# A windowed attention feeding a SoLU layer: two more tiles computed as a pair, their first sums on another engine, constants in one load, the last product in two halves

## The chip, the cores and the metric

The kernel runs on one core of one Trainium2 chip. The metric is the device time of one execution in microseconds (us). A core has TensorE (PE, with its weight loads shown apart as PEld), VectorE (DVE), ScalarE (ACT), GpSimd (POOL) and SyncE (SP, which here only issues transfers). Each takes its instructions in the order in which they were written, and waits at semaphores for the others.

## The reference

Attention in windows over 8 batches x 8 heads x 576 positions of 64 numbers, then a two-layer net with softmax-gated units over the 4608 rows that come out of it.

```python
scores = scale * q @ k.T                       # per batch and head
mask_plain = (rel >= 0) & (rel < 32)           # first 4 heads
mask_dil = (rel >= 0) & (rel < 128) & (rel % 4 == 0)   # last 4 heads
attn = softmax(where(mask, scores, -1e9))
x = (attn @ v) as rows of 512                  # 4608 x 512
h = x @ w_in                                   # 512 -> 1024
solu = h * softmax(h)
ln = (solu - mean) / sqrt(var + 1e-6) * g_ln
out = ln @ w_out                               # 1024 -> 512
```

## The kernel before

**Units and tiles.** The attention is cut into 32 units (two heads of one batch each), the net into 36 tiles of 128 rows. `scores` (L247 for the mask on TensorE, L255 for q with k), the softmax and `attend` (L333) make a unit; its x goes, transposed and split into a high and a low part, to a ring `x_hi`, `x_lo`. Products are made of three matmuls (high x high, high x low, low x high) in fp32r.

**Tiles.** Tiles 0 to 15 are computed singly: `moe_h` (L401) takes 24 matmuls of 512 columns for h, then maximum, exponential, gate, centring, variance. The result goes to DRAM and comes back so that it can be turned (L508 on VectorE), split (L516 on ScalarE, L522 on GpSimd) and multiplied with w_out (`moe_o`, L531, 24 matmuls of 512 columns per tile). Tiles 16 to 35 go in pairs: seven products P1 to P7 (`product`, L733, six matmuls each) replace the eight blocks of two tiles' h. They need sums of blocks of w_in (made once, words `fa` to `fh`, split by `Th`, `Tl`) and four sums S1 to S4 of blocks of x for each pair (`sums`, words z1 to z4; split by `hS12`, `hS34`, `lS12`, `lS34`). While the pair's rows are still in the ring (`in_ring`, tiles up to 17), x has a high and a low part, and S1 to S4 take 4, 2, 3 and 2 instructions; later one each where no batch boundary lies in the tile.

**Order.** No scheduler: the order on every engine is written out as words. `OPENING` covers the conversion of the weights, the first 12 units and tiles 0 to 5. Then `STEP` runs for each single tile i from 6 on (a step is h of tile i, scores of unit i+4, attend of unit i+3, w_out for tile i-2), with the words of `AMID` put behind its three parts in some steps. `PAIRED` is the first tile that is paired; from there `PAIR`, `PAIR_ALONE` and `LAST_PAIR` give the words for each pair, which also hold two units' attention and w_out of the two tiles before. `engine` gives z1 to z4, lS12 and lS34 to GpSimd.

**Loads.** All loads are issued by SP, in the order of the words. Each transfer takes the next of eight semaphores, and waits until the transfer eight places ahead of it, which had the same one, has landed.

**The end.** `LAST_PAIR` ends with the product of tile 35 with w_out, its eviction with the scale `rstd` in two halves (L548 on ScalarE, L551 on VectorE) and two stores.

Of the kernel before, what the change touches and what calls it, by code (L numbers as in the profile page):

```python
# [130 lines left out]
def windowed_attention_then_solu_kernel(  # L131
# [7 lines left out]
    g_ln: bass.AP,  # L139
    mask: bass.AP,  # L140
    ident: bass.AP,
    ident_bf: bass.AP,
# [20 lines left out]
    id_sb = const.tile([P, P], F32, name="id_sb")  # L163
    mask_sb = const.tile([P, 2, NS * WQ], BF16, name="mask_sb")
    g_sb = const.tile([P, FT], F32, name="g_sb")
    id_bf = const.tile([P, P], BF16, name="id_bf")
# [373 lines left out]
    def moe_out(i):  # L540
        ob = moe.tile([P, DO], F32, name="ob", bufs=1)
        rows, rstd = out[i * P : i * P + P, :], ms[i]["rstd"]
        if i < NTILE - 1:
            nc.scalar.activation(out=ob, in_=ps_o(i), func=AF.Copy, scale=rstd)  # L544
            nc.sync.dma_start(out=rows, in_=ob)
        else:
            left, right = slice(0, DO // 2), slice(DO // 2, DO)
# [3 lines left out]
            nc.vector.tensor_scalar(  # L551
                out=ob[:, right], in0=ps_o(i)[:, right], scalar1=rstd, scalar2=None, op0=ALU.mult
            )
            nc.scalar.dma_start(out=rows[:, left], in_=ob[:, left])
            nc.sync.dma_start(out=rows[:, right], in_=ob[:, right])
# [414 lines left out]
```

## Time and profile before

| | us |
|---|---|
| median of 3 runs (501.88, 503.55, 503.7) | 503.55 |
| the profiled execution | 504.69 |
| its span, first to last instruction | 502.8 |
| PE busy | 469.9 |
| DVE busy | 351.4 |
| POOL busy | 298.7 |
| ACT busy | 291.3 |

The profile is of one execution, slower by 1.14 than the median, and its span is 1.89 shorter than its own time. Busy time is how long an engine had an instruction in work; PE's ends are modelled. The slices of the page show when: PE starts slowly (1, 4, 5, 7 tenths in the first four of 40 slices), and from the seventh slice on is at 9 tenths until the last, which has 6. The transfer engines have 7 to 9 tenths in the first four slices.

### The profile page before, as it was taken

What the parts mean: (1) busy time and instruction counts of PE and PEld (TensorE: products, weight loads), DVE (VectorE), ACT (ScalarE), POOL (GpSimd) and SP (SyncE); (2) the same over time, 40 slices, a digit from 0 to 9 for tenths busy, and PEclk for the clock granted to TensorE, in tenths of its full rate; (3) what the DMA queues carried; (4) which work ended last, traced back from release to release, by engine and by line L of the source; (5) the groups of instructions that cost most, each with busy time, mean ns of one, the idle gap of its engine ahead of it and who ended that gap; (6) DMA issues with size and microseconds to landing.
All of it is one profiled execution on the core that took longest, in us unless ns stands there. A gap on an engine that the chain in (4) does not pass through costs nothing.

```text
span 502.8 us, 16542 instructions
## 1 busy us (share of the span) xinstructions
PE 469.9 (93%) x7064; PEld 376.0 (75%) x7064; DVE 351.4 (70%) x619; ACT 291.3 (58%) x483; POOL 298.7 (59%) x367
## 2 busy tenths in 40 slices
PE   1457998999999999999999999999999999999996
PEld 1336776788878888788878787878787888888875
DVE  3996989867627788777868686868676865445562
ACT  3766897744424444534457575757575767666551
POOL 1652776556533765778976666665756555766440
PEclk9999999999999999999999999999999999999999
DMA  7979175664465655666667677676765545354461
GB/s 280 402 254 359 37 261 163 230 190 133 137 193 156 194 164 169 186 175 178 201 175 216 206 211 211 210 211 211 212 210 164 160 129 146 104 168 124 113 188 63
DMA packets 51337, 94.14 MB, mean 187 GB/s; under 512 B 5952, under 2 KB 26048, under 8 KB 51264
## 3 DMA queue, kind: packets, MB, share of 16 engines
q1 hardware_dynamic: 50544, 92.43, 59.6%
q8 instruction: 55, 0.90, 0.8%
q10 hardware_dynamic: 720, 0.66, 0.4%
q14 instruction: 18, 0.15, 0.1%
HBM read 60.04 MB, written 28.31 MB: 176 GB/s over the span
## 4 chain that ended last, share of the span: by engine, by line
PE 91%; DMA 5%; issue 2%; DVE 1%; ACT 0%; SPq 0%; DVEq 0%; ACTq 0%
PE banks L531 40%; PE banks L733 20%; PE banks L401 18%; PE banks L333 7%; PE banks L255 6%; DMA qt<-qT 2%; DMA raw<-w_in 2%; DMA kt<-kT 1%; DVE pt L317 0%; PE banks L247 0%; DVE x_lo L388 0%; DVE nmax L412 0%; SPq L232 0%; DVE rs L302 0%; ACT sm L285 0%
## 5 line engine op out<-in xcount | busy, mean ns | idle before, releaser
L531 PE MATMUL banks<-w_o,th 128*128 128x512 f32 x576 | 179.9, 393 | 0.0
L522 POOL TENSOR_TENSOR tl<-t,th 128x512 fp32r<-128x512 f32 x68 | 87.9, 1305 | 59.9 <-ACT th L516 59.8
L531 PEld LDWEIGHTS banks<-w_o,th 128*128 128x128 f32 x576 | 106.6, 188 | 22.6 <-ACT th L516 0.6
L531 PE MATMUL banks<-w_o,tl 128*128 128x512 f32 x288 | 112.5, 391 | 0.0
L401 PE MATMUL banks<-w_i,x_hi 128*128 128x512 f32 x256 | 82.8, 405 | 0.2 <-DVE mu L436 0.2
L531 PEld LDWEIGHTS banks<-w_o,tl 128*128 128x128 f32 x288 | 54.0, 188 | 12.3 <-DVE tl L522 0.9
L516 ACT CAST th<-t 128x512 fp32r<-128x512 f32 x72 | 43.4, 621 | 23.5 <-DVE t L508 16.1
L401 PEld LDWEIGHTS banks<-w_i,x_hi 128*128 128x128 f32 x256 | 47.2, 191 | 11.1 <-DVE mu L436 0.8
L508 DVE STREAM_TRANSPOSE t<-raw 128x512 f32<-128x512 f32 x72 | 46.9, 684 | 6.1 <-DMA out<-ob 3.0
L401 PE MATMUL banks<-w_i,x_lo 128*128 128x512 f32 x128 | 50.7, 396 | 0.0
L333 PEld LDWEIGHTS banks<-pt,vt 32*64 32x64 f32 x2816 | 35.3, 138 | 20.0 <-issue 12.8
L452 ACT ACTIVATE e<-t 128x1024 f32<-128x1024 f32 x35 | 37.0, 1058 | 17.6 <-DVE t L448 17.3
L294 POOL TENSOR_TENSOR sm<-sm,mx 128x640 f32<-128x640 f32 x27 | 34.5, 1276 | 21.4 <-DVE mx L281 18.8
L333 PE MATMUL banks<-pt,vt 32*64 32x64 f32 (+3 forms) x2816 | 38.8, 234 | 8.6 <-issue 5.4
L298 ACT ACTIVATE sm<-sm 128x640 f32<-128x640 f32 x32 | 23.6, 739 | 35.8 <-POOL sm L294 35.1
L255 PEld LDWEIGHTS banks<-kt,qt 64*32 64x32 f32 x2560 | 29.8, 112 | 17.7 <-issue 10.7
L269 DVE TENSOR_TENSOR sm<-banks,mask_sb 128x640 f32<-128x640 f32 x22 | 18.1, 824 | 35.1 <-PE banks L255 35.0
L255 PE MATMUL banks<-kt,qt 64*32 64x64 f32 x2560 | 35.7, 238 | 5.6 <-issue 4.1
L544 ACT ACTIVATE ob<-banks,rstd 128x512 f32<-128x512 f32 x35 | 24.0, 686 | 24.8 <-issue 16.6
L757 DVE CUSTOM_DVE_ANT_0 t<-banks,t 128x512 f32<-128x512 f32 x30 | 20.7, 690 | 22.3 <-PE banks L733 16.9
L751 ACT COPY t<-banks 128x512 f32<-128x512 f32 x30 | 17.6, 588 | 30.3 <-PE banks L733 30.3
L427 ACT ACTIVATE e<-t,nmax 128x1024 f32<-128x1024 f32 x19 | 21.9, 1153 | 18.8 <-DVE nmax L764 18.2
(151 smaller groups left out, 868.5 us busy)
## 6 DMA issues: line engine op xcount, KB each, us to landing
mid<-t SPq DMA_DIRECT2D x140, 128.0 KB, 2.4
raw<-mid SPq DMA_DIRECT2D x34, 512.0 KB, 3.9
vt<-vw SPq DMA_DIRECT2D x32, 384.0 KB, 3.9
kt<-kT SPq DMA_DIRECT2D x32, 312.0 KB, 4.4
qt<-qT SPq DMA_DIRECT2D x32, 296.0 KB, 4.7
out<-ob SPq DMA_DIRECT2D x35, 256.0 KB, 2.7
x_hi<-x SPq DMA_DIRECT2D x12, 288.0 KB, 3.5
t<-w_in SPq DMA_DIRECT2D x5, 512.0 KB, 7.8
```

What stands on the lines that cost most here:

```text
L255: nc.tensor.matmul(out=ps[WIN * c : WIN * c + WIN, h, WQ * i : WQ * i + WQ], lhsT=qt[D * h : D * h + D, q0 : q0 + WIN], rhs=kt[D * h : D * ...
L294: eng.tensor_tensor(out=st[n]["sm"], in0=st[n]["sm"], in1=wide(mx), op=ALU.subtract)
L298: nc.scalar.activation(out=sm, in_=sm, func=AF.Exp, scale=0.125)
L333: nc.tensor.matmul(out=ps_x[D * h : D * h + D, c, c0 : c0 + k1 - k0], lhsT=vt[WIN * c : WIN * c + WIN, i, D * h : D * h + D], rhs=pt[WIN * ...
L401: nc.tensor.matmul(out=ps_h(i)[:, half], lhsT=a[:, kt, xs], rhs=w_i[:, kt, half, part, :], start=(kt == 0 and k == 0), stop=(kt == KT - 1 ...
L452: nc.scalar.activation(out=e, in_=t, func=AF.Square, accum_out=per_tile(i, "sq"))
L508: nc.vector.transpose(out=turned(i)[:, cut(c)].rearrange("p k (a r) -> p k a r", r=WIN), in_=ms[i]["mv"].rearrange("p (a k s) -> p k a s", ...
L516: nc.scalar.copy(out=ms[i]["th"][:, cut(c)], in_=turned(i)[:, cut(c)])
L522: eng.tensor_tensor(out=ms[i]["tl"][:, cut(c)], in0=turned(i)[:, cut(c)], in1=ms[i]["th"][:, cut(c)].bitcast(F32), op=ALU.subtract,)
L531: nc.tensor.matmul(out=ps_o(i), lhsT=a[:, f, :], rhs=w_o[:, f, part, :], start=(f == 0 and k == 0), stop=(f == FT - 1 and k == 2), skip_gr ...
L544: nc.scalar.activation(out=ob, in_=ps_o(i), func=AF.Copy, scale=rstd)
L733: nc.tensor.matmul(out=banks[:, bank], lhsT=left(pa, kt), rhs=right(pb, kt), start=j in (1, 2, 5) and kt == 0 and k == 0, stop=kt == 1 and ...
```

## The change

Five things, in the numbers and words that set the order, and in two functions.

1. `PAIRED` goes from 16 to 14: steps 14 and 15 fall away, tiles 14 and 15 become a pair in front of the other pairs. Their rows are in the ring.
2. The words of `AMID` start in step 8 instead of 9 and end in step 13 instead of 15.
3. In `sums`, S1 and S2 of the first pair go to VectorE; those of all others stay on GpSimd.
4. Four constants (bf16 identity, two masks, gains) lie in one array `pack` and are loaded by one transfer instead of four; the fp32 identity, which nothing read, is gone.
5. The product of tile 35 with w_out is made in two halves of 256 columns (`moe_o_half`), into two banks; the left half is evicted and stored while the right one is computed, and the right half is evicted in two quarters.

```diff
-PAIRED = 16
+PAIRED = 14
...
 AMID = {
-    9: ("fa0 fb0 fc0", "Th0", ""),
-    10: ("fd0 fe0 ff0", "Th4 Tl4 Tl0", ""),
-    11: ("fg0 fh0", "Th2 Tl2 Th6 Tl6", ""),
-    12: ("fa1 fb1 fc1", "Th1", ""),
-    13: ("fd1 fe1 ff1", "Th5 Tl5 Tl1", ""),
-    14: ("fg1 fh1 z1.s z2.s", "Th3 Tl3 Th7 Tl7", ""),
-    15: ("z3.s z4.s", "hS12.s lS12.s", "hS34.s lS34.s back.i"),
+    8: ("fa0 fb0 fc0", "Th0", "fd0"),
+    9: ("fe0 ff0", "Th4 Tl4 Tl0", "fg0 fh0"),
+    10: ("", "Th2 Tl2 Th6 Tl6", "fa1 fb1 fc1"),
+    11: ("fd1 fe1 ff1", "Th1 Th5 Tl5 Tl1", ""),
+    12: ("fg1 fh1", "Th3 Tl3 Th7 Tl7", "z1.s z2.s"),
+    13: ("z3.s z4.s", "hS12.s lS12.s", "hS34.s lS34.s back.i"),
 }
...
-    "w1 ib abs1 w3 m0 low1 q0 clamp1 w0 sign1 w2 abs3 q1 low3 q2 join1 hi1 S0 sign3 clamp3 "
+    "w1 pack abs1 w3 low1 q0 clamp1 w0 sign1 w2 abs3 q1 low3 q2 join1 hi1 S0 sign3 clamp3 join3 "
...
-    "oA.b oB.b out.b "
+    "oL.b outL.b oR.b outR.b "
...
-        a, b, eng = 2 * r, 2 * r + 1, engine(f"z{j}")
+        a, b = 2 * r, 2 * r + 1
+        eng = nc.vector if a == PAIRED and j <= 2 else engine(f"z{j}")
...
+    packed = const.tile([P, P // 2 + NS * WQ + FT], F32, name="packed")
+    id_bf = packed[:, 0 : P // 2].bitcast(BF16)
...
+    def moe_o_half(i, half):
+        th, tl = ms[i]["th"], ms[i]["tl"]
+        cols = slice(DO // 2 * half, DO // 2 * half + DO // 2)
+        for f in range(FT):
+            for k, (a, part) in enumerate(((th, 0), (th, 1), (tl, 0))):
+                nc.tensor.matmul(
+                    out=banks[:, half, cols],
+                    lhsT=a[:, f, :],
+                    rhs=w_o[:, f, part, cols],
...
+    def out_left(i):
+        moe_out_part(i, 0, slice(0, DO // 2), True)
+
+    def out_right(i):
+        moe_out_part(i, 1, slice(DO // 2, DO * 3 // 4), True)
+        moe_out_part(i, 1, slice(DO * 3 // 4, DO), False)
```

`moe_out_part(i, half, cols, on_act)` evicts the columns with the scale and stores them: on ScalarE with ScalarE's own queue, or on VectorE with SP's.

The order at three places follows. A name's number is its buffer, or a running count behind it; in square brackets stand the semaphores that an instruction waits for. Those named DMAHW0 to DMAHW7 are the eight that the transfers take in turn.

SP in the opening, before. Ahead of these rows stand t1 (the first block of w_in), the bf16 identity and t3 (the second block), with DMAHW0 to DMAHW2; t0, t2, raw4 and raw5 are further blocks of w_in, kt and qt the keys and queries of a unit:

```order
L835 DMA mask_sb_81<-mask 128x320
L209 DMA kt0_109<-kT 128x624
L210 DMA qt0_108<-qT 128x592
L232 DMA t0_113<-w_in 128x1024
L232 DMA t2_116<-w_in 128x1024
L209 DMA kt1_121<-kT 128x624 [waits DMAHW0_49]
L210 DMA qt1_120<-qT 128x592 [waits DMAHW1_49]
L209 DMA kt2_127<-kT 128x624 [waits DMAHW2_49]
L210 DMA qt2_126<-qT 128x592 [waits DMAHW3_49]
L232 DMA raw4_178<-w_in 128x1024 [waits DMAHW4_49]
L835 DMA mask_sb_81<-mask 128x320 [waits DMAHW5_49]
L232 DMA raw5_190<-w_in 128x1024 [waits DMAHW6_49]
```

And in the changed kernel, behind t1 with DMAHW0:

```order
L857 DMA packed_80<-pack 128x392
L228 DMA t3_100<-w_in 128x1024
L205 DMA kt0_105<-kT 128x624
L206 DMA qt0_104<-qT 128x592
L228 DMA t0_109<-w_in 128x1024
L228 DMA t2_112<-w_in 128x1024
L205 DMA kt1_117<-kT 128x624
L206 DMA qt1_116<-qT 128x592 [waits DMAHW0_49]
L205 DMA kt2_123<-kT 128x624 [waits DMAHW1_49]
L206 DMA qt2_122<-qT 128x592 [waits DMAHW2_49]
L228 DMA raw4_174<-w_in 128x1024 [waits DMAHW3_49]
L228 DMA raw5_185<-w_in 128x1024 [waits DMAHW4_49]
```

`packed` stands second and the two mask loads are gone. kt1 waits for nothing now, kt2 for `packed` instead of t3, raw4 for kt0 as before, raw5 for qt0 instead of t0.

VectorE at the end of step 12, before: x of unit 15, the end of unit 16's softmax, then the turns of tile 11 (`raw5` to `t3`) and the mask of unit 17:

```order
L388 TENSOR_TENSOR x_lo_89<-banks_90,x_hi_88 128x576
L312 TENSOR_TENSOR sm0_3009<-sm0_3009,rs_3074 128x640
L317 STREAM_TRANSPOSE pt0_3104<-sm0_3009 128x640
L508 STREAM_TRANSPOSE t3_2883<-raw5_2943 128x512 x2
L269 TENSOR_TENSOR sm1_3200<-banks_90,mask_sb_81 128x640
L281 TENSOR_REDUCE mx_3202<-sm1_3200 128x10
```

And in the changed kernel, where `mag3` and `low3` are the low parts of two sums of w_in and `qt3` holds S1 and S2:

```order
L384 TENSOR_TENSOR x_lo_86<-banks_87,x_hi_85 128x576
L308 TENSOR_TENSOR sm0_3015<-sm0_3015,rs_3079 128x640
L313 STREAM_TRANSPOSE pt0_3109<-sm0_3015 128x640
L588 TENSOR_TENSOR mag3_3112<-vt3_2339,more_2714 128x512
L588 TENSOR_TENSOR low3_3116<-kt3_2218,last_3114 128x512
L591 TENSOR_TENSOR qt3_2220<-x_hi_85 128x256
L591 TENSOR_TENSOR qt3_2220<-qt3_2220,x_lo_86 128x256 x2
L588 TENSOR_TENSOR qt3_2220<-qt3_2220,x_hi_85 128x256
L588 TENSOR_TENSOR qt3_2220<-qt3_2220,x_lo_86 128x256
L504 STREAM_TRANSPOSE t3_2890<-raw5_2949 128x512 x2
L265 TENSOR_TENSOR sm1_3216<-banks_87,packed_80 128x640
```

Two low parts and six instructions for S1 and S2 have come between the softmax of unit 16 and the turns of tile 11.

ScalarE behind the last split, and VectorE's last instruction, before: `ob` is what is stored, PE, Activation, DVE and Pool are the engines' semaphores:

```order
L516 CAST th1_6856<-t3_6696 128x512 [waits DVE_49]
L544 ACTIVATE ob_6887<-banks_90,rstd_6813 128x512 [waits PE_49,DMAHW0_49,Activation_49,Pool_49]
L548 ACTIVATE ob_6914<-banks_90,rstd_6813 128x256 [waits DMAHW1_49,PE_49,Activation_49]
L554 DMA out<-ob_6914 128x256 [waits DMAHW2_49,Activation_49]
L551 TENSOR_SCALAR ob_6914<-banks_90,rstd_6813 128x256 [waits DMAHW0_49,DMAHW1_49,Activation_49,Pool_49]
```

And in the changed kernel:

```order
L539 ACTIVATE ob_6889<-banks_87,rstd_6815 128x512 [waits PE_49,DMAHW4_49,Activation_49,Pool_49]
L566 ACTIVATE ob_6916<-banks_87,rstd_6815 128x256 [waits DMAHW5_49,PE_49,Activation_49]
L567 DMA out<-ob_6916 128x256 [waits DMAHW6_49,Activation_49]
L566 ACTIVATE sm1_6943<-banks_87,rstd_6815 128x128 [waits PE_49]
L567 DMA out<-sm1_6943 128x128 [waits DMAHW7_49,Activation_49]
L569 TENSOR_SCALAR sm0_6946<-banks_87,rstd_6815 128x128 [waits Activation_49,Pool_49]
```

ScalarE has a left half and a quarter to evict, and VectorE's quarter waits for ScalarE's semaphore as its half did.

## Rows read from the trace of the kernel before

**Rows 1.** The page: the span, the busy time of each engine with its share and count of instructions (section 1), and the chain that ended last by engine (section 4).

```profile
span 502.8 us, 16542 instructions
...
PE 469.9 (93%) x7064; PEld 376.0 (75%) x7064; DVE 351.4 (70%) x619; ACT 291.3 (58%) x483; POOL 298.7 (59%) x367
...
PE 91%; DMA 5%; issue 2%; DVE 1%; ACT 0%; SPq 0%; DVEq 0%; ACTq 0%
```

**Rows 2.** The table of stages: from and to, length, then busy us and count of PE, PEld, DVE, ACT and POOL, granted clock, share of the transfer engines, GB/s.

```profile
12.00:26.40 14.40, 6.75 (x262) 4.51 (x261) 14.00 (x25) 10.80 (x18) 8.14 (x6) 1.00 1.03 402
26.40:42.90 16.50, 7.69 (x339) 6.17 (x339) 14.17 (x23) 8.97 (x15) 9.65 (x7) 1.00 0.84 286
...
62.00:82.00 20.00, 17.56 (x446) 13.58 (x448) 17.02 (x32) 17.15 (x30) 14.55 (x25) 1.00 0.69 216
...
140.00:254.00 114.00, 113.93 (x1833) 91.45 (x1831) 84.81 (x127) 51.64 (x87) 78.28 (x103) 1.00 0.61 181
254.00:404.00 150.00, 150.00 (x2547) 120.39 (x2545) 111.59 (x215) 95.09 (x159) 96.76 (x109) 1.00 0.66 197
```

**Rows 3.** The chain of work that ended last, in order of time, in the opening: start us, us, what.

```profile
17.39 9.02 DMA qt<-qT
...
26.97 2.98 issue
...
32.47 2.56 issue
...
38.61 2.83 issue
...
42.91 4.48 PE banks L401 x12
```

**Rows 4.** The timeline of the opening: start us, us, engine, line, instruction, and in brackets the idle time before it with what ended it.

```profile
1.17 0.42 SPq L833 DMA_DIRECT2D id_bf<-ident_bf  x1
...
8.58 0.33 SPq L209 DMA_DIRECT2D kt<-kT  x1
8.58 0.66 ACT L780 ACTIVATE mag<-t 128x512 f32<-128x512 f32 x1 [2.75 <-DMA t<-w_in]
...
11.65 0.33 SPq L232 DMA_DIRECT2D raw<-w_in  x1
...
14.00 0.69 PE L247 MATMUL banks<-mask_sb,id_bf 128*128 128x320 bf16 x2 [2.12 <-DVE sm L291]
```

**Rows 5.** The page, section 3: a DMA queue, its packets, MB and share of 16 engines. This is the queue that brings instructions.

```profile
q8 instruction: 55, 0.90, 0.8%
```

**Rows 6.** The chain again: two products of 320 columns, six products of a pair, and the 24 of one tile with w_out.

```profile
51.35 0.29 PE banks L247 x2
...
268.83 1.36 PE banks L733 x6
270.19 5.44 PE banks L531 x24
```

**Rows 7.** The table of stages, columns as in rows 2: step 12, step 15 and the first pair (tiles 16 and 17).

```profile
197.77:211.10 13.33, 13.33 (x210) 10.71 (x209) 11.16 (x18) 6.38 (x12) 9.59 (x12) 1.00 0.59 174
...
238.23:251.56 13.33, 13.33 (x210) 10.71 (x209) 11.29 (x18) 6.67 (x13) 12.05 (x19) 1.00 0.67 201
251.56:276.76 25.20, 25.20 (x428) 20.22 (x426) 18.51 (x37) 16.04 (x27) 17.46 (x20) 1.00 0.66 196
```

**Rows 8.** The timelines of single engines: VectorE and GpSimd in step 13, TensorE in step 13, then GpSimd and TensorE in the first pair.

```profile
211.76 1.26 DVE L508 STREAM_TRANSPOSE t<-raw 128x512 f32<-128x512 f32 x2
...
213.16 2.53 POOL L522 TENSOR_TENSOR tl<-t,th 128x512 fp32r<-128x512 f32 x2 [1.14 <-ACT th L516]
...
219.60 0.39 PE L531 MATMUL banks<-w_o,tl 128*128 128x512 f32 x1
...
264.42 2.56 POOL L522 TENSOR_TENSOR tl<-t,th 128x512 fp32r<-128x512 f32 x2 [1.49 <-ACT th L516]
...
270.48 0.39 PE L531 MATMUL banks<-w_o,tl 128*128 128x512 f32 x1
```

**Rows 9.** Groups of instructions by line and shape: count, then busy us and mean ns of one, then idle us before them.

```profile
L531 PEld LDWEIGHTS banks<-w_o,tl 128*128 128x128 f32 x288 | 54.0, 188 | 12.3 <-DVE tl L522 0.9
...
L544 ACT ACTIVATE ob<-banks,rstd 128x512 f32<-128x512 f32 x35 | 24.0, 686 | 24.8 <-issue 16.6 <-DMA out<-ob 4.2 <-PE banks L531 3.9
...
L564 DVE TENSOR_TENSOR vt<-x_hi,vt 128x256 fp32r<-128x256 f32 x6 | 4.4, 726 | 0.0
...
L567 POOL TENSOR_TENSOR kt<-kt,x_lo 128x256 f32<-128x256 f32 x2 | 1.5, 742 | 0.2
...
L564 DVE TENSOR_TENSOR mag<-vt,more 128x512 fp32r<-128x512 f32 x2 | 1.3, 652 | 0.0
...
L564 DVE TENSOR_TENSOR x_lo<-x_hi,x_lo 128x256 fp32r<-128x256 f32 x1 | 0.4, 383 | 0.0
```

**Rows 10.** The timeline of the end: two weight loads at the start of the last product, and the two evictions behind it.

```profile
492.77 0.30 PEld L531 LDWEIGHTS banks<-w_o,th 128*128 128x128 f32 x2 [0.17 <-ACT th L516]
...
498.90 0.47 ACT L548 ACTIVATE ob<-banks,rstd 128x256 f32<-128x256 f32 x1 [5.02 <-PE banks L531]
...
499.47 0.48 DVE L551 TENSOR_SCALAR ob<-banks,rstd 128x256 f32<-128x256 f32 x1 [5.43 <-ACT ob L548]
```

**Rows 11.** DMA issues of the whole run: KB each and median us from issue to landing.

```profile
out<-ob ACTq DMA_DIRECT2D x1, 128.0 KB, 1.8
```

More of the change, by code (lines that the diff above doesn't have):

```diff
@@ L138, in windowed_attention_then_solu_kernel @@
     w_out: bass.AP,
[L139 to L142, printed above, removed]
+    pack: bass.AP,
     out: bass.AP,
@@ L161, in windowed_attention_then_solu_kernel @@
     )
[L163 to L166, printed above, removed]
+    packed = const.tile([P, P // 2 + NS * WQ + FT], F32, name="packed")
+    id_bf = packed[:, 0 : P // 2].bitcast(BF16)
+    mask_sb = packed[:, P // 2 : P // 2 + NS * WQ].bitcast(BF16).rearrange("p (d c) -> p d c", d=2)
+    g_sb = packed[:, P // 2 + NS * WQ :]
     mhalf = const.tile([P, 1], F32, name="mhalf")
@@ L542, in moe_out @@
         rows, rstd = out[i * P : i * P + P, :], ms[i]["rstd"]
-        if i < NTILE - 1:
-            nc.scalar.activation(out=ob, in_=ps_o(i), func=AF.Copy, scale=rstd)
-            nc.sync.dma_start(out=rows, in_=ob)
-        else:
-            left, right = slice(0, DO // 2), slice(DO // 2, DO)
-            nc.scalar.activation(
-                out=ob[:, left], in_=ps_o(i)[:, left], func=AF.Copy, scale=rstd
-            )
[L551 to L555, printed above, removed]
+        nc.scalar.activation(out=ob, in_=ps_o(i), func=AF.Copy, scale=rstd)
@@ new lines, in moe_out @@
+        nc.sync.dma_start(out=rows, in_=ob)
+        del ms[i]
+    def moe_o_half(i, half):
[7 more added lines that the diff above has]
+                    rhs=w_o[:, f, part, cols],
+                    start=(f == 0 and k == 0),
+                    stop=(f == FT - 1 and k == 2),
+                    skip_group_check=True,
+                )
@@ new lines, in moe_out_part @@
+    def moe_out_part(i, half, cols, on_act):
+        if half == 0:
+            ob = moe.tile([P, DO], F32, name="ob", bufs=1)
+        else:
+            ob = att.tile([P, 2, NS, WQ], F32, name=f"sm{int(on_act)}")
+            ob = ob.rearrange("p h s w -> p (h s w)")
+        rows, rstd = out[i * P : i * P + P, :], ms[i]["rstd"]
+        ps = banks[:, half]
+        if on_act:
+            nc.scalar.activation(out=ob[:, cols], in_=ps[:, cols], func=AF.Copy, scale=rstd)
+            nc.scalar.dma_start(out=rows[:, cols], in_=ob[:, cols])
+        else:
+            nc.vector.tensor_scalar(
+                out=ob[:, cols], in0=ps[:, cols], scalar1=rstd, scalar2=None, op0=ALU.mult
+            )
+            nc.sync.dma_start(out=rows[:, cols], in_=ob[:, cols])
@@ L831, in windowed_attention_then_solu_kernel @@
         "q": load_qk, "v": load_v, "w": load_w,
-        "i": lambda _: nc.sync.dma_start(out=id_sb, in_=ident),
-        "ib": lambda _: nc.sync.dma_start(out=id_bf, in_=ident_bf),
-        "g": lambda _: nc.sync.dma_start(out=g_sb, in_=g_ln),
-        "m": lambda d: nc.sync.dma_start(out=mask_sb[:, d], in_=mask[:, d]),
+        "pack": lambda _: nc.sync.dma_start(out=packed, in_=pack),
         "abs": conv_abs, "low": conv_low, "clamp": conv_clamp, "sign": conv_sign,
@@ L849, in windowed_attention_then_solu_kernel @@
         "oA": lambda i: moe_o(i, range(FT // 2)), "oB": lambda i: moe_o(i, range(FT // 2, FT)),
+        "oL": lambda i: moe_o_half(i, 0), "oR": lambda i: moe_o_half(i, 1),
+        "outL": out_left, "outR": out_right,
         "xf": spread_hi, "xd": move_x, "pk": peak_of,
@@ L952 @@
         "w_out": _bits(_by_blocks(inputs["moe_w_out"]).reshape(DF, DO)),
-        "g_ln": np.ascontiguousarray(_by_blocks(inputs["moe_g_ln"]).reshape(FT, P).T),
-        "mask": _mask().astype(ml_dtypes.bfloat16),
-        "ident": np.eye(P, dtype=np.float32),
-        "ident_bf": np.eye(P, dtype=np.float32).astype(ml_dtypes.bfloat16),
+        "pack": np.concatenate(
+            [
+                np.eye(P, dtype=ml_dtypes.bfloat16).view(np.float32),
+                _mask().astype(ml_dtypes.bfloat16).reshape(P, -1).view(np.float32),
+                np.ascontiguousarray(_by_blocks(inputs["moe_g_ln"]).reshape(FT, P).T),
+            ],
+            axis=1,
+        ),
     }
```

26 rows, old and new, of the table OPENING are left out of this document.

## The prediction

> **What bounds the kernel now.** I read the page's busy times and chain first. TensorE is busy for 469.9 of 502.8 us and 91% of the chain that ended last is its own work [rows 1]. The table of stages shows where it is not busy: before 42.9, a little between 62 and 82 (17.56 of 20.00), and nearly nowhere in the two long stretches behind (113.93 of 114.00, 150.00 of 150.00) [rows 2]. So the kernel has three parts. In the opening TensorE waits, and the chain is made of transfers and of "issue" [rows 3]. In the middle only fewer or shorter TensorE instructions count, as long as nobody else comes late. At the end a short chain of eviction and store follows the last product [rows 10].
>
> **Tiles 14 and 15 as a pair.** Two tiles computed singly take 2 x 24 products of x with w_in, a pair takes 7 x 6 = 42: six of 512 columns fewer. A product of the pair (six matmuls) takes 1.36 on the chain [rows 6], so this term is **-1.36 us**. Cross-check: two steps of 13.33 make 26.66, and the first pair takes 25.20 [rows 7]: 1.46 less, of which the attention pieces in them explain a little. The term is all on the path, since TensorE has no gap there.
>
> What it costs elsewhere must be hidden. GpSimd does the sums of w_in one or two steps earlier, so its fullest single steps change places; before, the fullest was step 15 with 12.05 of 13.33 and TensorE lost nothing in it [rows 7]. In after, the fullest is step 13, with the same S3, S4 and their low parts. Then the pair of 14 and 15 carries the sums of 16 and 17, which are still in the ring and so are 11 instructions instead of the 4 that stood in the first pair before: 7 x 0.742 = 5.2 us more on GpSimd [rows 9], 17.46 + 5.2 = 22.7 of 25.20 [rows 7]. Two of these come ahead of the low parts of the second tile: 264.42 + 2.56 + 1.5 = 268.5 in the before's clock, and TensorE asks for the first of them at 270.48 [rows 8]. That still fits.
>
> VectorE gets S1 and S2 at the end of step 12, behind two low parts of w_in. The order shows that the two turns of tile 11 stand right behind them. The nearest rows for one sum of 128x256 are 0.383 and 0.726 [rows 9]; I take 0.42, because the slow row reads together with a busy GpSimd, and get 6 x 0.42 = 2.5, with 2 x 0.65 for the low parts 3.8 us (at the slow price 5.7). The turns move from 211.76 to about 215.6. Their high part and the low part on GpSimd follow: the first low part was ready 213.16 + 1.27 = 214.4 and would be at about 218.3, and TensorE reads it at 219.60 [rows 8]. So **0**, with 1.3 us to spare, and up to +0.6 at the slow price. Queued behind on VectorE are the mask and the maximum of unit 17; TensorE needs that unit only in the middle of the pair. A gain is excluded here, because TensorE has nothing to win in a stretch without gaps.
>
> **The last product by halves.** The last tile's product was 24 matmuls of 512 columns, 5.44 [rows 6], and becomes 48 of 256. No row shows fp32r matmuls of 256 columns. From 512 columns (5.44/24 = 0.227 each) and 320 (0.29/2 = 0.145 each) [rows 6] a column costs 0.000427 and 256 columns 0.118. A weight load of 128 columns must fit beside each: two in a row took 0.30 where one takes 0.188, so they follow at 0.112 [rows 9, 10], just under 0.118. I take 48 x 0.118 = 5.66, **+0.22**; lower bound 48 x 0.112 = 5.38 (-0.06), upper bound one full load time each, 48 x 0.188 = 9.02 (+3.6). The value lies near the lower end because loads and products already overlap in every row of 512 columns: 0.188 of load within 0.227.
>
> The gain is in the drain. Before, ScalarE's half took 0.47 and VectorE's 0.48 one after the other, though they don't touch the same columns [rows 10]. In after the left half leaves while the right one is computed, but the order shows that VectorE's quarter again waits for ScalarE's. So both remain in a row, each by 128 columns shorter: 0.686 for 512 columns and 0.474 for 256 make 0.106 per 128 [rows 9, 10], twice that is **-0.21**. The last store carries 64 KB instead of 128 KB, which took 1.8 [rows 11]: I take **-0.1** (0 to -0.3). The end together: -0.1, from -0.6 to +3.3.
>
> [...] Rows show a load of 0.188 within each pace of 0.227, so loads run beside products. [...]
>
> **Constants in one load.** Five loads become one of 196 KB, the second on SP's queue. Ahead of the second block of w_in stand 196 KB instead of 32 KB: 164 KB at the 402 GB/s of 12 to 26.4 [rows 2] are 0.4 us. ScalarE waits for that block at 8.58, and through VectorE the scores of unit 1 wait for it at 14.00 [rows 4]: up to +0.4. Against it: after the first five blocks the bytes ahead are the same, one issue of 0.42 falls away before the first q and k, and since each load waits for the one eight places ahead of it on the queue (order), the third pair of k and q no longer waits until 8.58 and the later block of w_in until 11.65 [rows 4]. But from 12 to 26.4 the transfer engines are full (1.03) [rows 2], and an earlier issue there lands no earlier. I take **-0.2**, half an issue slot.
>
> What follows is coarser. From 27 to 42 TensorE waits three times for "issue", 2.98, 2.56 and 2.83 [rows 3], and the queue for instructions moved 0.90 MB in 55 pieces [rows 5], 16 KB each. I read them as waits for the program itself, which comes through the same transfer engines as the loads. A shift in the loads can shorten or lengthen any of them, so the bounds of this term are -2.3 and +2.3: one such wait, cut to VectorE's idle time in that stretch (16.50 - 14.17) [rows 2], since VectorE would be late next.
>
> [...]
>
> **Sum.** -1.36 + 0 - 0.1 - 0.2 = -1.66. The profiled execution took 504.69 (span 502.8, 1.9 around it), so it would take 503.0. It is 1.1 above the median of the three runs, 503.55, mostly a matter of one execution against another; the same difference from the median gives **501.9 us**, -0.33%. That is inside 0.5% (2.5 us), about what a measurement of this kernel can tell from no change.
>
> **The rivals.** (1) *The opening gives more*: one wait for instructions falls away, because bulk loads drain earlier. -2.3 in place of -0.2 gives 499.8. For it: three waits on the path. Against: the bytes and their rate are the same. (2) *The opening loses*: with the small constants gone the eight loads in flight are all large, a wait for instructions grows, and the second block of w_in lands later. +2.3 in place of -0.2: 504.4; TensorE's 2.4 idle us between 62 and 82 would take up some of it. (3) *VectorE or GpSimd late in steps 12 and 13*: at 0.726 a sum TensorE stalls by 0.6, with a late unit 17 by 1.5: 502.5 to 503.4. (4) *The weight loads go in series with half-width products*: 0.112 + 0.118 = 0.23 each, 48 x 0.23 = 11.0, +5.6 in place of +0.22: 507.3, slower. It decides from a pace of 0.205 on: there 48 x 0.205 - 5.44 = 4.4, 4.2 more than in the sum, and the kernel stands 0.5% above before. For it: no row has this width. Against: the 0.112 of loads in a row.
>
> **How the numbers follow.** Forecast 0.55, with a range of its own from 500.9 to 502.9; rival 1 0.20, rival 2 0.12, rival 3 0.08, rival 4 0.05. The range for 8 in 10 takes in the forecast, rival 3, nearly all of rival 1 and most of rival 2, and leaves out rival 4: 499.7 to 504.2. Faster by over 0.5% means below 501.0: rival 1 without its weakest part, 0.17, and the lower tail of the forecast, 0.13, together 0.30. Slower by over 0.5% means above 506.1: rival 4 and a little of rival 2, 0.06. The rest, 0.64, lies within 0.5%.
>
> **What would show it.** Steps 14 and 15 gone and a stretch of about 25.2 to 25.5 in their place, without idle time on TensorE; if it stalls at the last tile product of step 13, VectorE's sums were too dear. The last 48 matmuls at 0.118 each; 0.19 means loads, 0.23 series. VectorE's last quarter starting after ScalarE's. In the opening the start of the first product of x with w_in, 42.9 now [rows 3]: 42.7 by the sum, under 41 by rival 1, over 44 by rival 2. The prediction is wrong in its main term if TensorE's busy time after 82 doesn't fall by about 1.4 less 0.2.

## The result, and the profile after

The changed kernel takes **506.33 us** (median of 6 runs, 505.42 to 507.02) where the kernel before takes 503.12 (6 runs, 501.8 to 503.81): a ratio of 1.0066, 95% interval 1.0047 to 1.0086. It is slower, and lies above the range of the prediction. Its profiled execution took 505.91, span 503.7.

The page after, chain by engine (section 4), beside [rows 1]:

```profile
PE 75%; DVE 12%; POOL 4%; DMA 3%; issue 3%; ACT 2%; SPq 0%; DVEq 0%; ACTq 0%; POOLq 0%
```

TensorE's share of the chain falls from 91% to 75%: somewhere the end is set by VectorE and GpSimd. The table of stages after, columns as in [rows 2], finds the place:

```profile
140.00:254.00 114.00, 110.25 (x1812) 87.53 (x1811) 86.01 (x137) 54.36 (x92) 82.06 (x103) 1.00 0.56 167
254.00:404.00 150.00, 150.00 (x2470) 120.14 (x2468) 111.51 (x215) 95.39 (x160) 95.96 (x108) 1.00 0.68 201
```

Before, TensorE was busy for 113.93 of the same 114 us [rows 2]; now it idles for 3.75 of them, all ahead of the end of the first pair (columns 1 and 2: 114.00 long, 110.25 busy). The waits of TensorE after (waited for, us in total, times, longest):

```profile
PE banks L758 <- ACT ob L539: 2.0, 1, 2.0
PE banks L329 <- DVE sm L265: 1.3, 1, 1.3
PE banks L397 <- DVE mu L432: 0.4, 1, 0.4
```

In order of time: 0.4 ahead of products with w_in (behind a gate), 1.3 in the attend of unit 16 (behind the mask of unit 17), 2.0 ahead of the second product of the pair (behind ScalarE's eviction of tile 11, which reads the bank that this product writes). The chain of after, in order of time, shows what leads to the last (start us, us, what):

```profile
184.19 1.30 POOL kt L591
185.49 1.25 POOL qt L591
...
186.81 1.31 POOL qt L588
188.12 2.48 POOL tl L518 x2
190.61 1.23 POOL sm L290
...
191.86 0.75 ACT sm L294
...
193.48 1.01 DVE rs L302
...
194.73 1.08 DVE t L432
...
196.04 0.77 DVE t L444
...
197.19 2.47 DMA mid<-t
...
201.75 2.52 POOL tl L518 x2
...
213.92 0.35 DVE qt L591
...
216.01 0.71 DVE t L504
...
217.44 2.52 POOL tl L518 x2
...
223.78 1.08 DVE t L432
...
227.60 0.59 ACT ob L539
```

This is a loop that closes once a step: low parts on GpSimd, the subtraction behind them (L290), the exponential on ScalarE, softmax sums, gate (L432) and centre (L444) on VectorE, the rest of VectorE's queue up to the next turn (L504), the rounding on ScalarE (L512), low parts again. At 197.19 the chain goes by a transfer to memory, but the timeline shows VectorE without a gap over that time, so its queue alone carries the lateness on:

```profile
196.71 0.75 DVE L384 TENSOR_TENSOR x_lo<-banks,x_hi 128x576 fp32r<-128x576 f32 x1
197.38 0.82 DVE L308 TENSOR_TENSOR sm<-sm,rs 128x640 f32<-128x640 f32 x1
198.23 0.85 DVE L313 STREAM_TRANSPOSE pt<-sm 128x640 f32<-128x640 f32 x1
199.11 0.69 DVE L588 TENSOR_TENSOR low<-kt,kt 128x512 fp32r<-128x512 f32 x1
199.71 0.68 DVE L588 TENSOR_TENSOR mag<-qt,tp 128x512 fp32r<-128x512 f32 x1
```

The rounds of the loop begin at 188.12, 201.75 and 217.44, so they take 13.6 and 15.7 us for steps that TensorE could do in 13.33 [rows 7]. Three sums of w_in (184.19 to 188.12) stand ahead of the first round.

Executions differ in the opening (see the constants, below), so I compare one stretch by the timelines of TensorE: from the attend of step 8 (unit 11) to the attend of unit 19 in the pair of tiles 16 and 17. Its two ends, before and then after:

```profile
150.67 1.08 PE L333 MATMUL banks<-pt,vt 32*64 32x64 f32 x80
262.08 1.08 PE L333 MATMUL banks<-pt,vt 32*64 32x64 f32 x80
...
148.34 1.08 PE L329 MATMUL banks<-pt,vt 32*64 32x64 f32 x80
263.12 1.08 PE L329 MATMUL banks<-pt,vt 32*64 32x64 f32 x80
```

Before the stretch takes **111.41 us**, after **114.78**. Three kernels below without the pair part take 111.2 to 111.8, so a difference of less than some 0.5 us says little; each figure is of one execution. The gap in the spans is then -2.33 (opening) + 3.37 (this stretch) - 0.14 (rest) = +0.90. The two profiled executions are 1.2 apart in time and the medians 3.2, because the one of before was 1.6 above its median (504.69 to 503.12) and that of after 0.4 below.

### The profile page after: what moved, and what is told of

It reads as the page before. It is cut to its first block, busy times and chain, and to the rows that moved or that the text cites. A ratio compares the mean times of both kernels' runs of the same rounds, so it can differ in the third digit from the quotient of the medians.

```text
span 503.7 us, 16600 instructions
## 1 busy us (share of the span) xinstructions
PE 470.3 (93%) x7082; PEld 376.3 (75%) x7082; DVE 354.1 (70%) x630; ACT 295.2 (59%) x491; POOL 302.8 (60%) x368
## 4 chain that ended last, share of the span: by engine, by line
PE 75%; DVE 12%; POOL 4%; DMA 3%; issue 3%; ACT 2%; SPq 0%; DVEq 0%; ACTq 0%; POOLq 0%
PE banks L527 31%; PE banks L758 22%; PE banks L397 12%; PE banks L329 5%; PE banks L251 4%; POOL tl L518 2%; DVE rs L298 2%; DMA mid<-t 2%; DVE t L432 1%; PE banks L548 1%; DMA t<-w_in 1%; DVE mag L836 1%; DVE low L828 1%; POOL sm L290 1%; DVE rs L302 1%
## 5 line engine op out<-in xcount | busy, mean ns | idle before, releaser
L527 PE MATMUL banks<-w_o,th 128*128 128x512 f32 x560 | 174.8, 393 | 0.0
L527 PEld LDWEIGHTS banks<-w_o,th 128*128 128x128 f32 x560 | 103.6, 188 | 21.9 <-ACT th L512 0.4
L527 PE MATMUL banks<-w_o,tl 128*128 128x512 f32 x280 | 109.2, 390 | 0.0
L397 PE MATMUL banks<-w_i,x_hi 128*128 128x512 f32 x224 | 73.0, 407 | 0.6 <-DVE mu L432 0.6
L512 ACT CAST th<-t 128x512 fp32r<-128x512 f32 x72 | 43.3, 621 | 25.2 <-DVE t L504 18.2
L504 DVE STREAM_TRANSPOSE t<-raw 128x512 f32<-128x512 f32 x72 | 47.0, 685 | 7.3 <-DMA raw<-mid 6.4
L397 PEld LDWEIGHTS banks<-w_i,x_hi 128*128 128x128 f32 x224 | 41.2, 191 | 10.9 <-DVE mu L432 2.0
L290 POOL TENSOR_TENSOR sm<-sm,mx 128x640 f32<-128x640 f32 x27 | 34.5, 1276 | 19.8 <-DVE mx L277 16.8
L397 PE MATMUL banks<-w_i,x_lo 128*128 128x512 f32 x112 | 44.4, 397 | 0.0
L265 DVE TENSOR_TENSOR sm<-banks,packed 128x640 f32<-128x640 f32 x22 | 18.1, 821 | 31.9 <-PE banks L251 31.8
L776 ACT COPY t<-banks 128x512 f32<-128x512 f32 x33 | 19.4, 588 | 33.9 <-PE banks L758 33.9
L782 DVE CUSTOM_DVE_ANT_0 t<-banks,t 128x512 f32<-128x512 f32 x33 | 22.8, 690 | 22.0 <-PE banks L758 16.6
L423 ACT ACTIVATE e<-t,nmax 128x1024 f32<-128x1024 f32 x21 | 24.2, 1152 | 21.1 <-DVE nmax L789 20.5
```

The costliest lines, as they stand in the source:

```text
L290: eng.tensor_tensor(out=st[n]["sm"], in0=st[n]["sm"], in1=wide(mx), op=ALU.subtract)
L397: nc.tensor.matmul(out=ps_h(i)[:, half], lhsT=a[:, kt, xs], rhs=w_i[:, kt, half, part, :], start=(kt == 0 and k == 0), stop=(kt == KT - 1 ...
L423: nc.scalar.activation(out=e, in_=h, func=AF.Exp, bias=nmax, scale=1.0, accum_out=se)
L504: nc.vector.transpose(out=turned(i)[:, cut(c)].rearrange("p k (a r) -> p k a r", r=WIN), in_=ms[i]["mv"].rearrange("p (a k s) -> p k a s", ...
L512: nc.scalar.copy(out=ms[i]["th"][:, cut(c)], in_=turned(i)[:, cut(c)])
L527: nc.tensor.matmul(out=ps_o(i), lhsT=a[:, f, :], rhs=w_o[:, f, part, :], start=(f == 0 and k == 0), stop=(f == FT - 1 and k == 2), skip_gr ...
```

## The experiments

My first theory: words at the end of a step (the third column of AMID) stand on GpSimd and VectorE ahead of the next step's low parts, turns, masks and subtraction. (a) The sums of w_in at the ends of steps 9 and 10 make the gates late; (b) S1 and S2 on VectorE at the end of step 12 make the mask of unit 17 and the gate of tile 13 late. Rivals: the amount of work in these steps, wherever it stands; or another part of the change.

**The parts alone.** *e1_const*, the load of constants in the kernel before:

```diff
-        "ib": lambda _: nc.sync.dma_start(out=id_bf, in_=ident_bf),
...
+        "pack": lambda _: nc.sync.dma_start(out=packed, in_=pack),
```

> The kernel before with the constants in one load alone. Theory A (the opening gains what the changed kernel's trace shows, its first product of x with w_in starting at 40.06 instead of 42.91 us, and the loss lies in the steps ahead of the new pair): about -2.3 us against before, the first product at about 40.1, and nothing lost later. Rival (the earlier opening is a chance of one execution, or is given back in the middle, where the other engines don't come earlier): within 0.7 us of before.

*e2_tail*, the last product by halves in the kernel before:

```diff
-    "oA.b oB.b out.b "
+    "oL.b outL.b oR.b outR.b "
```

> The kernel before with the last product by halves alone. From the changed kernel's trace the 48 matmuls follow at 0.120 us, 5.76 instead of 5.44, and from the end of the last one to the end of the span it is 3.3 instead of 4.0: -0.4 us. Rival (the halves cost more because the left one must wait for the low part of the last tile): 0 to +0.5 us.

*e3_pair*, the pair part in the kernel before: PAIRED, AMID and the engine of S1 and S2.

```diff
-PAIRED = 16
+PAIRED = 14
...
+        eng = nc.vector if a == PAIRED and j <= 2 else engine(f"z{j}")
```

> The kernel before with the third pair part of the change alone: tiles 14 and 15 as a pair, the sums of w_in from step 8, S1 and S2 on VectorE; constants and last product as before. Theory A (the whole loss is here): 4.5 us of waits against 1.4 saved, and the 1.1 that the end lost with it, so +3 to +5.5 us against before. Rival (the loss needs the earlier opening, TensorE running ahead of the engines that serve it): 0 to +2 us.

*e4_const_tail*, the edits of e1 and e2 together.

> The kernel before with constants in one load and the last product by halves, no new pair. Theory A: the two gains add, -2.7 us against before, faster than both kernels. Rival (the opening's gain is given back): within 0.7 us.

Before took 503.12 on this chip (25 runs). Measured: e1 502.33, ratio 0.9993 (0.9968 to 1.0019); e2 501.79, 0.9982 (0.9954 to 1.001); e4 503.42, 0.9995 (0.997 to 1.002); e3 **507.78, 1.0089** (1.0055 to 1.0124). (The ratios are not those of the medians and differ a little from them.) The loss is in the pair part alone; the stretch of e3 is 114.74. It is made otherwise than in after: its waits are 1.3, 0.4 and 0.3, and some 1.7 us more went to a fall of TensorE's clock (last section).

**Place or engine.** *e5_sums_behind*:

```diff
-    12: ("fg1 fh1", "Th3 Tl3 Th7 Tl7", "z1.s z2.s"),
-    13: ("z3.s z4.s", "hS12.s lS12.s", "hS34.s lS34.s back.i"),
+    12: ("fg1 fh1", "Th3 Tl3 Th7 Tl7", ""),
+    13: ("z1.s z2.s z3.s z4.s", "hS12.s lS12.s", "hS34.s lS34.s back.i"),
```

> The changed kernel with S1 and S2 of the first pair still on VectorE, but issued in step 13 behind the two turns of t and the mask and maximum of unit 17, not at the end of step 12. Theory (place in the order): TensorE's 1.33 us before the attend of unit 16 and most of its 2.01 us before the second product of the pair go; the span falls by 2 to 3.3 us against the changed kernel's 503.7, so 500.4 to 501.7, and the median of the runs lies at 503 to 504.3. Rival (amount of work: VectorE and GpSimd have more to do in these steps wherever it stands): the waits move but their sum stays within 0.7 us, a median of 505.6 to 507.

Measured 509.71, 1.0149 (1.0114 to 1.0184) of before's 502.44 (19 runs): slower still. The stretch is 117.09, of which some 1.3 us are a fall of the clock (last section). The attend no longer waits, but the second product waits 4.5 us. The timeline of VectorE in e5 and in after shows one reason:

```profile
215.87 1.46 DVE L591 TENSOR_TENSOR qt<-x_hi 128x256 f32<-128x256 f32 x1
217.37 2.26 DVE L591 TENSOR_TENSOR qt<-qt,x_lo 128x256 f32<-128x256 f32 x2
219.66 0.84 DVE L588 TENSOR_TENSOR qt<-qt,x_hi 128x256 f32<-128x256 f32 x1
```

```profile
213.84 0.42 DVE L591 TENSOR_TENSOR qt<-x_hi 128x256 f32<-128x256 f32 x1
214.29 0.88 DVE L591 TENSOR_TENSOR qt<-qt,x_lo 128x256 f32<-128x256 f32 x2
215.21 0.43 DVE L588 TENSOR_TENSOR qt<-qt,x_hi 128x256 f32<-128x256 f32 x1
```

The same sums cost 2 to 3.5 times as much in e5, where GpSimd works beside them (in after it idles from 213 to 217.4). And moving them behind the mask only moves the wait: the gate of tile 13 is behind them either way. Part (b) of the theory, as a matter of place, fell.

*e6_places_only*, the kernel before with the sums of w_in in the changed kernel's places (S1 to S4 as before):

```diff
-    9: ("fa0 fb0 fc0", "Th0", ""),
-    10: ("fd0 fe0 ff0", "Th4 Tl4 Tl0", ""),
...
+    8: ("fa0 fb0 fc0", "Th0", "fd0"),
+    9: ("fe0 ff0", "Th4 Tl4 Tl0", "fg0 fh0"),
+    10: ("", "Th2 Tl2 Th6 Tl6", "fa1 fb1 fc1"),
+    11: ("fd1 fe1 ff1", "Th1 Th5 Tl5 Tl1", ""),
+    12: ("fg1 fh1", "Th3 Tl3 Th7 Tl7", ""),
```

> The kernel before (pairs from tile 16 on) with the sums of w_in in the places that the changed kernel gives them (steps 8 to 12, three of them at the ends of steps 9 and 10); S1 to S4 stay on GpSimd in steps 14 and 15. Theory (sums at the end of a step stand ahead of the next step's low parts and softmax on GpSimd): the steps 10 to 13 lose 0.7 to 1.2 us, with short waits of TensorE for the banks of h behind the gate of VectorE, and the attend of step 13 starts that much later; median 503.8 to 504.4 where before has 503.1. Rival (all of the loss comes from S1 and S2 on VectorE): within 0.3 us of before.

Measured 503.23, 1.0025 (1.0 to 1.005); stretch 112.41, **+1.0**, all of it between the attends of steps 10 and 13, with 0.4 behind a gate. Part (a), as expected in kind and size.

*e7_sums_dve_only*, the kernel before with S1 and S2 on VectorE:

```diff
-    14: ("fg1 fh1 z1.s z2.s", "Th3 Tl3 Th7 Tl7", ""),
+    14: ("fg1 fh1", "Th3 Tl3 Th7 Tl7", "z1.s z2.s"),
```

> The kernel before (pairs from tile 16 on) with one edit: S1 and S2 of the first pair on VectorE at the end of step 14, behind the last two low parts of the weights' sums, where it had them on GpSimd in step 14. Theory: the attend in step 15 waits 1 to 1.4 us for the mask of the unit behind it, and the second product of the pair 1.5 to 2 us for the eviction of the tile before; 2.4 to 3.4 us in all, a median of 505.5 to 506.5, and some 2 us more where the granted clock falls after the first of the waits. Rival (the loss needs the earlier pair, so two steps less for the same work): 0 to 0.5 us, a median of 503 to 503.7.

Measured 503.18, 1.0044 (1.0013 to 1.0074); stretch 112.78, **+1.4**, half of the expected, with one wait of 1.0 ahead of the second product; the expected wait of the attend did not come. The two edits apart make 2.4; in after they make 3.37 + 1.36 (the six matmuls saved) = 4.7.

*e8_early_pool*: nothing at the ends of steps, the sums of w_in from step 6, S1 to S4 on GpSimd.

```diff
+    6: ("fa0 fb0 fc0", "Th0", ""),
+    7: ("fd0 fe0 ff0", "Tl0 Th4 Tl4", ""),
+    8: ("fg0 fh0", "Th2 Tl2 Th6 Tl6", ""),
...
+    13: ("z1.s z2.s z3.s z4.s", "hS12.s lS12.s", "hS34.s lS34.s back.i"),
```

> The changed kernel with every word of the third slots moved: the sums of w_in stand behind the subtraction in steps 6 to 11, three or two to a step (two of the scratch values get places of their own so that they can begin two steps earlier), none at the end of a step; S1 to S4 are on GpSimd behind the subtraction of step 13. Theory: none of the four waits of TensorE between 195 and 229 us is left above 0.3 us, the span falls by 4 to 5 us to 498.7 to 499.7, the median to 500.7 to 502, 0.995 to 0.998 of before. Rival (amount of work): GpSimd has 7.4 us of sums in step 13 and the pair starts late by 1 to 3 us; median 503 to 505.

Measured 512.96, 1.0209 (1.0169 to 1.0249). A flaw of my own hides the answer: most of steps 6 and 7 is already done in the opening, so six sums stood together on GpSimd (149.15 to 157.2). VectorE's low parts waited for them, the mask of the next unit (157.71) stood behind these low parts, and the attend of step 8 waited 7.7 us for that mask. The next step ran in part at a granted clock of 0.50; the later ones took 13.3 to 13.5 without a wait, and the pair waited 0.9 for the low part of S1 and S2.

**The loop.** New theory: lateness is carried round the loop and along the in-order queues to the eviction that the second product waits for. *e9_rearranged* uses the hole at the end of the opening, keeps the ends of steps free, and shares S1 to S4 between the engines (two scratch values get places of their own):

```diff
-    "norm11 thB6 xh10 xl10 v13 q13 var7 out4 tlA6 back7 tlB6 out5 "
+    "norm11 thB6 fa0 fb0 fc0 Th0 fd0 fe0 Tl0 Th4 ff0 Tl4 xh10 xl10 v13 q13 var7 out4 tlA6 back7 tlB6 out5 "
...
+    8: ("fg0 fh0", "Th2 Tl2 Th6 Tl6", ""),
+    9: ("fa1 fb1 fc1", "Th1", ""),
+    10: ("fd1 fe1 ff1", "Tl1 Th5 Tl5", ""),
+    11: ("fg1 fh1", "Th3 Tl3 Th7 Tl7", ""),
+    13: ("z1.s z2.s", "hS12.s lS12.s z3.s z4.s", "hS34.s lS34.s back.i"),
...
+        eng = nc.vector if a == PAIRED and j >= 3 else engine(f"z{j}")
```

> The changed kernel with the third slots emptied once more. The first five sums of w_in, and the two rounded and two low parts made from them, go to the end of the opening, ahead of the copy of x of unit 10, where the trace of before shows GpSimd idle from 137.4 to 145.5 us and VectorE from 137 to 144.5; the other sums stand behind the subtraction in steps 8 to 11. In step 13 S1 and S2 are on GpSimd behind the subtraction, S3 and S4 on VectorE behind the turn of unit 17. Theory (lateness is carried by the queues of VectorE, GpSimd and ScalarE, each in order, to the eviction that the second product of the pair waits for): no wait of TensorE above 0.3 us from step 8 to the end of the first pair, the pair's 1.36 us are kept, the span is 499.5 to 501 when the first product with w_in starts at 41 to 42 us, and the median 500.2 to 502, a ratio of 0.994 to 0.998. Rival (a pair two tiles earlier costs something that no order of these words removes): a ratio of 1.000 to 1.005.

Measured **501.56, 0.9976** (0.9953 to 1.0) of before's 501.95 (31 runs). The table of stages of e9:

```profile
140.00:254.00 114.00, 113.95 (x1889) 91.43 (x1890) 88.67 (x139) 56.30 (x94) 82.73 (x105) 1.00 0.62 180
```

No wait is left in it; the stretch is 109.98, **-1.43** against before. GpSimd and VectorE are as busy there as in after (82.73 to 82.06, 88.67 to 86.01): busy time was not what counted.

*e10_sums_pool*, the changed kernel with S1 and S2 on GpSimd in step 13 (AMID as in e5):

```diff
-        eng = nc.vector if a == PAIRED and j <= 2 else engine(f"z{j}")
+        eng = engine(f"z{j}")
```

> The changed kernel with S1 and S2 of the first pair on GpSimd, behind the subtraction of step 13, with S3 and S4; the sums of w_in as changed. Theory (what matters is how late VectorE comes to the gate of tile 13, and through it ScalarE to the eviction of tile 11): the 1.33 us before the attend of unit 16 goes, the 2.0 us before the second product falls to 0 to 0.8, and up to 1 us appears before the product of S1, whose low part is now 7 us of GpSimd later; the median 503.8 to 505.2. Rival (work done late anywhere costs the same): 505.6 to 507.

Measured 507.01, 1.0088 (1.0055 to 1.0121), a miss; stretch 114.50. Its waits:

```profile
PE banks L758 <- ACT ob L539: 1.9, 1, 1.9
PE banks L758 <- POOL w_i L588: 1.1, 1, 1.1
```

Without S1 and S2 on VectorE the attend's wait goes, but the wait for the eviction stays. The eviction does come sooner: 9.4 us after the start of the attend of unit 16 (216.17 to 225.59), where after has 11.1 (216.43 to 227.51). But TensorE, which no longer waits in the attend, asks for it 1.6 sooner too. So S1 and S2 are part of the lateness and not all of it.

*e11_early_sums_dve*, the sums of w_in as in e9, S1 to S4 as changed:

```diff
+    12: ("", "", "z1.s z2.s"),
+    13: ("z3.s z4.s", "hS12.s lS12.s", "hS34.s lS34.s back.i"),
```

> The changed kernel with its sums of w_in at the end of the opening and in steps 8 to 11 as in the rearranged kernel, but with S1 and S2 on VectorE at the end of step 12 and S3 and S4 on GpSimd in step 13, as changed. Theory: the steps 9 to 12 lose nothing; VectorE has no lateness ahead of S1 and S2, so the wait before the attend of unit 16 is at most 0.3 us and the one before the second product 0.7 to 1.5 us (1.0 where the same edit was made alone in the kernel before); the median 502.6 to 504.2. Rival (the two waits come from S1 and S2 alone, in full): 1.3 and 2.0 us as in the changed kernel, 505 to 506.

Measured 501.61, 0.9997 (0.9971 to 1.0022); stretch 110.15, with none of the two waits, better than I expected. So S1 and S2 on VectorE cost nothing in this order, where the loop is on time and their step has no other words for w_in; in before's order they cost 1.4 (e7).

*e12_evict_first*, the changed kernel with the squares of tile 13 behind the eviction of tile 11 on ScalarE, and with them the rounding and the low part of S1 and S2:

```diff
-    13: ("z3.s z4.s", "hS12.s lS12.s", "hS34.s lS34.s back.i"),
+    13: ("z3.s z4.s", "", "var.i hS12.s lS12.s hS34.s lS34.s back.i"),
...
+            run(part.replace("var.i ", "") if i == PAIRED - 1 else part, of, done)
```

> The changed kernel with one edit in step 13: the sum of squares of tile 13 stands behind the eviction of tile 11 on ScalarE, not ahead of it. Theory (the second product of the pair waits for that eviction only because ScalarE's queue holds it behind the squares of a late tile 13): the wait of 2.0 us falls to 0 to 0.3 us, and 0.5 to 1.2 us of it come back before the product of S1, whose rounding waits on the same queue; the attend's 1.33 us stays; the median 504.8 to 505.8. Rival (the product waits for something else that ends at the same time, such as the gate's read of its banks): the 2.0 us stays, 506 to 507.

Measured 505.53, 1.0061 (1.0035 to 1.0087); stretch 113.12, 1.7 less than after. Its waits:

```profile
PE banks L329 <- DVE sm L265: 1.3, 1, 1.3
PE banks L397 <- DVE mu L432: 0.5, 1, 0.5
PE banks L758 <- POOL w_i L588: 0.4, 1, 0.4
```

The 2.0 is gone, 0.4 comes back, the rest stays: the eviction was held by ScalarE's order behind a late tile 13.

**Place or amount.** e9 and e11 changed both. *e13_first_slots* keeps all sixteen sums in steps 8 to 12, each behind the subtraction of its step; *e14_few_third_slots* takes five out and puts the rest at the ends. Both give two scratch values places of their own, as e9 does:

```diff
+    8: ("fa0 fb0 fc0 fd0", "Th0", ""),
+    9: ("fe0 ff0 fg0", "Th4 Tl4 Tl0", ""),
+    10: ("fh0 fa1 fb1", "Th2 Tl2 Th6 Tl6", ""),
+    11: ("fc1 fd1 fe1", "Th1 Th5 Tl5 Tl1", ""),
+    12: ("ff1 fg1 fh1", "Th3 Tl3 Th7 Tl7", "z1.s z2.s"),
```

> The changed kernel with all sixteen sums of w_in still in steps 8 to 12, but each behind the subtraction of its step and none at the end of one (two scratch values get places of their own, so that no sum waits for a low part); S1 to S4 as changed. GpSimd has the same work in the same five steps. From the attend of step 8 to the first attend after the pair the changed kernel takes 114.8 us, the rearranged ones 110.0 and 110.2. Theory (place: sums at the end of a step stand ahead of the low parts and the softmax of the next one): 110 to 111.3 us, no wait above 0.5 us, median 501.3 to 503. Rival (amount: sixteen sums in five steps are too much for GpSimd beside the rest): 113.5 to 115 us and 505 to 506.5.

```diff
+    7: ("", "", "fg0 fh0"),
+    8: ("", "Th2 Tl2 Th6 Tl6", "fa1 fb1 fc1"),
+    9: ("", "Th1", "fd1 fe1 ff1"),
+    10: ("", "Tl1 Th5 Tl5", "fg1 fh1"),
+    11: ("", "Th3 Tl3 Th7 Tl7", ""),
```

> The other half of the cross: five sums of w_in and two pairs of rounded and low parts at the end of the opening, and the remaining eleven at the ends of steps 7 to 10, none behind a subtraction; S1 to S4 as changed. Less work in the steps than the changed kernel, in the worse place. The same stretch: by the theory (place) 112 to 114.5 us with waits for banks of h behind the gate and for the eviction before the second product, median 503 to 505.5; by the rival (amount) 110 to 111 us, median 501 to 503.

Measured: e13 503.02, 1.0018 (0.9993 to 1.0043); e14 506.66, 1.0075 (1.0048 to 1.0101); before 502.23 (15 runs). The ends of the stretch in e13, e14 and e11:

```profile
148.88 1.08 PE L329 MATMUL banks<-pt,vt 32*64 32x64 f32 x80
260.70 1.08 PE L329 MATMUL banks<-pt,vt 32*64 32x64 f32 x80
...
148.39 1.08 PE L330 MATMUL banks<-pt,vt 32*64 32x64 f32 x80
264.28 1.08 PE L330 MATMUL banks<-pt,vt 32*64 32x64 f32 x80
...
148.44 1.08 PE L329 MATMUL banks<-pt,vt 32*64 32x64 f32 x80
258.59 1.08 PE L329 MATMUL banks<-pt,vt 32*64 32x64 f32 x80
```

The stretch of the four:

| sums of w_in | sixteen in steps 8 to 12 | five of them in the opening |
|---|---|---|
| some or all at the ends of steps | after 114.78 | e14 115.89 |
| all behind the subtraction | e13 111.82 | e11 110.15 |

Place decides: 3.0 us between after and e13, 5.7 between e14 and e11. Of the 5.7 some 1.3 (an estimate, last section) are a fall of the clock that of these four only e14 has, so 4.4 are left. Fewer sums give 1.7 in the good place and, without that fall, 0.2 in the bad one. The place acts in two ways that these runs don't part: sums ahead of the low parts hold them up, and in after and e14 alike GpSimd first stands idle for 1.07 us (until 184.19 and 188.25), since a sum there overwrites a value that VectorE's low part still reads; in e13 no sum waits so. e13 still waits 0.9 for the eviction, so the amount is a second, smaller cause. e14 came out worse than either expectation.

*e15_pair_rearranged*, PAIRED, OPENING, AMID and engines as in e9, in the kernel before; no other part:

```diff
-PAIRED = 16
+PAIRED = 14
```

> The kernel before with the pair part alone, in the rearranged order: pairs from tile 14 on, the first five sums of w_in at the end of the opening, the others behind the subtraction in steps 8 to 11, S1 and S2 on GpSimd and S3 and S4 on VectorE in step 13; five loads of constants and the last product whole, as before. Theory (the pair pays its six matmuls once nothing late reaches it): from the attend of step 8 to the first attend after the pair 110.0 to 110.2 us where before has 111.4, no wait of TensorE above 0.3 us between, median 1.2 to 1.5 us below before on the same chip, a ratio of 0.997 to 0.998. Rival (the gain seen with the other two parts came from them): 1.000 and over, with the same stretch at 111 us or more.

Measured 503.44, 1.0008 (0.9977 to 1.0038) of before's 502.83 (17 runs); stretch 110.01, **-1.40**. The trace bears the theory out; the timed runs, which scatter from 500.6 to 506.4, can't tell 1.4 us from nothing.

## Why the prediction was wrong

**The pair, -1.36: right.** Where nothing late reaches it the stretch is shorter by 1.40 (e15) and 1.43 (e9). The sign that the prediction named for this term, TensorE's busy time after 82 us, doesn't serve, since after is 2.3 ahead at that point. Over the stretch the busy time is 111.34 before, 111.03 after and 109.93 in e9; where the 1.1 between after and e9 go, beyond the idle time, is not shown.

**The step that failed is "What it costs elsewhere must be hidden", with its result 0, up to +0.6.** It cost 4.7: the stretch should have been 1.36 shorter and was 3.37 longer. Two readings in it were wrong. It judged GpSimd by the busy time of the fullest step, and so said nothing of the sums of w_in that now stood at the ends of steps 9 and 10, ahead of the low parts and the subtraction; e13 against after shows that this place costs 3.0. And it placed the turns of tile 11 at 215.6 by the timetable of before: they came at 216.01, which is 218.3 in before's clock (2.33 later), since VectorE was already late when S1 and S2 began: it started to turn the softmax of unit 16 (L313) at 211.90, 3.2 later than before did in that clock. The price of a sum, 0.42, was right. Their number was not: the text ahead of the prediction counts six instructions for S1 and S2, the timeline has five, and with the two low parts they took 3.3 and not 3.8. For the same reason the four sums take 10 instructions and not 11, and 22.7 on GpSimd should be 21.9; neither moves the result. The sentence that TensorE needs unit 17 only in the middle of the pair was wrong too: the attend of unit 16 waited 1.3 for its mask. And the eviction of tile 11, for which the second product waits, was not in the argument; e12 shows it.

**Rival 3** named the place and who would be late, at 0.6 to 1.5 and a chance of 0.08. Its reason, dear sums, was not the one (they took 0.42), and it had a third of the size at most, because it counted one late arrival and not a loop that carries lateness from step to step.

**The last product, +0.22 - 0.21 - 0.1.** The chain at the end of after:

```profile
494.67 5.78 PE banks L548 x46
...
500.47 0.38 ACT sm L566
...
500.94 0.35 DVE sm L569
```

The timeline has three half products every 0.36 us, 0.120 each for the 0.118 of the estimate, so rival 4 falls: the weight loads (L548 on PEld), 0.19 each, keep the same pace beside the products, three in 0.36. That the estimate came so near is in part luck: its row of 320 columns is of bf16 products [rows 4], and these are fp32r. ScalarE's and VectorE's quarters stand one after the other, as said. From the attend of the last unit to the end of the span it is 90.3 after and 90.5 before: about the forecast, and not to be seen in the time (e2).

**Constants, -0.2, within 2.3.** The first product with w_in starts at 40.06 in after and at 42.91 before [rows 3], which looks like rival 1. But over all profiled executions it starts at 38.1 to 42.6 (mean 39.9, eleven with one load) and at 39.0 to 42.8 (mean 41.7, six with five loads), and the timed e1 is at 0.9993. Its interval leaves anything open from a gain of 1.6 us to a loss of 1.0. The reading of the three waits for "issue" [rows 3] as waits for instructions has this for it: the only three packets of the queue of [rows 5] between 20 and 45 us lie one in each, from 27.4, 32.8 and 39.1 on, 1.0 to 1.1 long (DMA view of before).

## What to carry to other kernels

Where engines pass work round once a step, follow the chain for one turn and compare its length with the step: here queues that were 72% (GpSimd) and 75% (VectorE) busy had no room ahead of the link that the next engine waits for, and room behind it. Cost a moved instruction at its place in its in-order queue, with what then stands behind it, in a timetable that already holds the other moves. When runs scatter by more than the effect, compare one stretch between two landmarks in the traces.
